# A transformer block in float32 halves: where GpSimd's elementwise work stands in the order

## Chip, cores and metric

One NeuronCore of a Trainium2 chip runs the whole kernel. The metric is the device time of one execution in microseconds, as the median of several runs.

## What is computed

A transformer block with adaptive layer norm, for one batch of 2048 rows of 512 values, all in float32. Six vectors of 512 come from the condition `c`; they scale, shift and gate.

```python
mod = (silu(c) @ w_mod).reshape(1, 6, 1, -1)
sa, ca, ga, sb, cb, gb = six vectors of mod
h = layernorm(x) * (1 + ca) + sa
q, k, v = split(h @ wqkv)                  # 32 heads of 16
p = softmax(q @ k.T * 16 ** -0.5)
x = x + ga * ((p @ v) @ wo)
h = layernorm(x) * (1 + cb) + sb
u = h @ w1 + b1                            # 1792 wide
x = x + gb * ((u * tanh(softplus(u))) @ w2)
```

## The kernel before

**Float32 products from parts.** A matrix product runs as three products of fp32r operands: each operand is split into a high part (a copy rounded to fp32r, `hi_copy`) and a low part (the rest, `lo_sub`), and high x high, high x low and low x high are added up in PSUM. So each intermediate that enters a product is split first, by a copy and a subtraction, mostly on GpSimd (`eng="p"`).

**Attention sets the beat.** The rows are cut into four query blocks of 512, the heads into eight groups of four: 32 iterations n = 8 qb + g. Each iteration has sixteen steps, T = 512 steps in all, and each step works on 128 keys: four products of scores (L506), their exponentials on ScalarE (L514, tile `pr`), the product with the values two steps later (L534), and, for a later iteration, four products (L470) whose row maxima VectorE reduces (L472, `mx`). Scores and maxima go through a ring of six PSUM banks. Each step is two half steps h = 2t and 2t + 1.

**An order written out by hand.** The schedule is manual: every engine runs its instructions in the order in which the program emits them. `at(h, f)` puts a function on the list of half step h, and the lists are run in order, each in the order in which it was filled. So "+13" says where an instruction stands in its engine's queue, not when it runs; what runs later is set by the waits. `clear(h)` only moves a half step out of a stretch of each iteration. SP issues all the transfers, in order; GpSimd runs its work in order too.

**Units beside the attention.** The other products are cut into units that are queued in a fixed order (`queue`) and emitted a few at a time beside the scores, on half the rows of the array each. A unit's `fin(h)` follows its last product and hangs the elementwise stages on the half steps behind it. There are these kinds:

- `qk_unit` projects 128 columns of q or k for 512 rows. ScalarE copies the bank into `ql` (L242), GpSimd makes the high part `qh` (L95) and turns `ql` into the low part (L98). `put`, some half steps later, stores them to DRAM in the layout in which the pairs of heads are loaded: for q two stores of `qh` and one of `ql` (L252), for k one of `qh` written twice (L256) and one of `ql` (L257). `qh` and `ql` have two buffers each. These units lie ahead of iteration 7's end.
- The MLP of query block qb, from iteration 8 (qb + 1) on: `wo_unit` (attention output, four row blocks), `tr_unit` (transposes after the layer norm), fourteen `up_unit` f = 0 to 13 (128 columns of the 1792 each, a slice), and `down_unit` (the product with w2 for a group of slices and 128 rows; its sum is added to `y` on GpSimd, L879, out of one buffer `yd`). In the order, slices 0 to 4 follow one another, slices 5 to 8 alternate with the first group's `down_unit`, of six products, and later slices with wider ones. An `up_unit` takes eight half steps, the first group's `down_unit` four. The fourth query block's MLP is a tail of its own.

**A slice's stages** (`mish`), for a unit whose `fin` is at h, outside the tail: bias on ScalarE (L728, tile `hb`), clamp on GpSimd (L734, into `ee`), exponential on ScalarE (L740), a product of two instructions on GpSimd (L748, L749), logarithm and inverse on ScalarE (L752, L755), the quotient of five instructions on GpSimd (L764 to L768), `place` (no instruction) and the split into `a_h` and `a_l` on GpSimd (L95, L98). The half steps behind h are in the list that the diff changes, from clamp to split.

**A group of heads is finished** in `evac(n)`, called at the end of step t1 = 16 (n + 1) + 1: ScalarE copies the accumulator to `ot` (L548). The sums of the exponentials go by DMA to `sm` (L559, `sums`), the four heads' rows to half of `od` (L563, `rows`), VectorE takes the reciprocal `rc` (L569), SP stores it to DRAM (`rscr`, L570) and loads it back, spread over the rows (`rb`, L572). When two groups (a pair, g odd) are there, GpSimd multiplies (L578) and splits the result into `o_hl` (L95, L98), which `wo_unit` reads. `od` and `rb` have one buffer each. With `hurry` (g = 7, the block's last heads) the steps stand closer, and the three instructions on one half step.

The order in the lists decides also what stands beside these: a pair of heads' k and q (`load_pair`, L293 and L302) at half step 32 (n - 2) + 9 or 15 and at 32 (n - 1), the values (L457), wo's four quarters for the next block (`w<-woscr`, L660, two of them when the fourth group's last unit is done), and the stores of the row maxima into `qa` (L495) at 32 n - 5.

Of the kernel before, what the change touches and what calls it, by code (L numbers as in the profile page):

```python
# [8 lines left out]
F32 = mybir.dt.float32  # L9
# [9 lines left out]
def adaln_block(ctx: ExitStack, tc: tile.TileContext, x, wqkv, wo, w1, b1, w2, c, w_mod, out):  # L19
    nc = tc.nc  # L20
    P = 128
    S, D = x.shape[1], x.shape[2]
# [5 lines left out]
    TB = 512  # L28
# [32 lines left out]
    rscr = dram.tile([NIT, 4, TB], F32, name="rscr")  # L61
# [24 lines left out]
    def dap(t, off, ap):  # L86
        return bass.AP(tensor=t.tensor, offset=t.offset + off, ap=ap)

    def hi_copy(eng, hi, src):
        if eng == "a":  # L90
            nc.scalar.copy(hi, src)
        elif eng == "v":
            nc.vector.tensor_copy(hi, src)
        else:
            nc.gpsimd.tensor_scalar(hi, src, 1.0, 0.0, op0=ALU.mult, op1=ALU.add)  # L95

    def lo_sub(eng, lo, src, hi):
        (nc.gpsimd if eng == "p" else nc.vector).tensor_sub(lo, src, hi.bitcast(F32))  # L98
# [12 lines left out]
    def mm3(acc, ah, al, bh, bl, late="a"):  # L111

        n = len(ah)
        seq = ((ah, bh), (ah, bl), (al, bh)) if late == "a" else ((ah, bh), (al, bh), (ah, bl))
        seq = [(l[k], r[k]) for l, r in seq for k in range(n)]
        for i, (l, r) in enumerate(seq):
            mm(acc, l, r, i == 0, i == len(seq) - 1)
# [36 lines left out]
    def bank(tag="ms"):  # L154
        return ring() if tag == "ring" else ps.tile([P, TB], F32, tag=tag, name="bk", bufs=1)
# [25 lines left out]
    def clear(h):  # L181

        return h if h < 60 or h % 32 < 25 else h - h % 32 + 34

    def at(h, f):

        hooks.setdefault(h, []).append(f)
# [38 lines left out]
    def qk_unit(kind, ct, tb, tag):  # L226

        wh, wl = slices[kind, ct]
        acc = bank(tag)
        ts_ = slice(tb * TB, (tb + 1) * TB)  # L230
        mm3(acc, [wh[:, k, :] for k in range(DK)], [wl[:, k, :] for k in range(DK)],
            [h_h[:, k, ts_] for k in range(DK)], [h_l[:, k, ts_] for k in range(DK)], "b")

        def fin(h=None):
            qh = qp.tile([P, TB], F32R, tag="qh", name="qh", bufs=2)
            ql = qp.tile([P, TB], F32R, tag="ql", name="ql", bufs=2)
            if h is None:
                hi_copy("a", qh, acc)
                lo_sub("v", ql, acc, qh)
            else:  # L240
                qf = ql.bitcast(F32)
                nc.scalar.copy(qf, acc)  # L242
                hi_copy("p", qh, qf)
                lo_sub("p", ql, qf, qh)
            scr, rows = (qscr, 50) if kind == 0 else (kscr, 48)

            def put():
                put_away.add((kind, ct, tb))
                o = 8 * ct * rows * S + tb * TB
                if kind == 0:  # L250
                    for r, src in enumerate((qh, qh, ql)):
                        nc.sync.dma_start(dap(scr, o + r * S, [[rows * S, 8], [3 * S, DH], [1, TB]]), src.bitcast(F32))  # L252
                    return
                hi = qh.bitcast(F32)
                twice = bass.AP(tensor=hi.tensor, offset=hi.offset, ap=[list(hi.ap)[0], [0, 2], [1, TB]])
                nc.sync.dma_start(dap(scr, o, [[3 * S, P], [2 * S, 2], [1, TB]]), twice)  # L256
                nc.sync.dma_start(dap(scr, o + S, [[3 * S, P], [1, TB]]), ql.bitcast(F32))  # L257

            put() if h is None else at(clear(h + (5 if h > 60 else 2)), put)
        return fin  # L260
# [265 lines left out]
    def pv(t):  # L526
        if not 0 <= t < T:
            return
        n, kc = divmod(t, 16)
        if kc == 0:  # L530
            accs[n] = bank("acc")
        for h in range(4):
            o = (kc * 4 + h) * VW
            nc.tensor.matmul(accs[n][32 * h:32 * h + 32, :], vgs[n][:, o:o + 32], pts.pop((t, h)),  # L534
                             start=(kc == 0), stop=(kc == 15))
        if kc == 15:
            evac(n)
# [4 lines left out]
    def evac(n):  # L542
        qb, g = divmod(n, G)
        t1 = 16 * (n + 1) + 1
        if g == 0:
            o_hl[qb] = [ap.tile([P, DK, TB], F32R, tag=f"o_{i}", name="o_hl", bufs=1) for i in range(2)]
        ot = ap.tile([P, TB], F32, tag="ot", name="ot", bufs=1)
        nc.scalar.copy(ot, accs.pop(n))  # L548
        if g % 2 == 0:
            st["od"] = ap.tile([P, TB], F32, tag="od", name="od", bufs=1)  # L550
            st["rb"] = ap.tile([P, TB], F32, tag="rb", name="rb", bufs=1)
        od, rb = st["od"], st["rb"]
        b = 64 * (g % 2)
        if n == NIT - 1:
            mst["last"] = (ot, od, rb)
            return
        sm = ap.tile([P, 16], F32, tag="sm", name="sm", bufs=2)
        def sums():
            nc.sync.dma_start(sm, ot[DH::32, :])  # L559

        def rows():
            for h in range(4):
                nc.sync.dma_start(od[b + 16 * h:b + 16 * h + 16, :], ot[32 * h:32 * h + DH, :])  # L563

        rc = ap.tile([P, 16], F32, tag="rc", name="rc", bufs=2)
        hurry = g == G - 1
        at(2 * t1 + 2, sums)
        at(2 * t1 + 3, rows)
        at(2 * t1 + (10 if hurry else 12), lambda: nc.vector.reciprocal(rc, sm))  # L569
        at(2 * t1 + (11 if hurry else 13), lambda: nc.sync.dma_start(rscr[n], rc))  # L570
        at(2 * t1 + (13 if hurry else 17),
           lambda: nc.sync.dma_start(rb[b:b + 64, :], dap(rscr, n * 4 * TB, [[TB, 4], [0, DH], [1, TB]])))  # L572
        if g % 2 == 1 or n == NIT - 2:
            r = slice(0, P if g % 2 else 64)

            oh, ol = o_hl[qb]
            k, d = 2 * t1 + (29 if g == 1 else 17 if hurry else 23), 0 if hurry else 2
            at(k, lambda: nc.gpsimd.tensor_mul(od[r], od[r], rb[r]))  # L578
            at(k + d, lambda: hi_copy("p", oh[r, g // 2, :], od[r]))
            at(k + 2 * d, lambda: lo_sub("p", ol[r, g // 2, :], od[r], oh[r, g // 2, :]))  # L580
# [85 lines left out]
    def load_w1(f):  # L666
        return load_split("w1", 2, w1scr[f])
# [42 lines left out]
    def up_mms(acc, w, hh, hl):  # L710
        mm3(acc, [w1v(w, 0, k) for k in range(DK)], [w1v(w, 1, k) for k in range(DK)],
            [hh[:, k, :] for k in range(DK)], [hl[:, k, :] for k in range(DK)], "b")
# [67 lines left out]
    def idle(h):  # L780

        return h is not None and 2 * (T - PRO) + 2 < h <= 2 * T
# [5 lines left out]
    def block(qb, t0):  # L788
# [60 lines left out]
        def up_unit(f, tag):  # L849
            w = w1s.pop(f)  # L850
            acc = bank(tag)
            up_mms(acc, w, *hx)
            act[f], (bias, *stages) = mish(f, acc, False)

            def fin(h):
                bias(idle(h))
                for i, s in zip((1, 3, 4, 9, 13, 13, 16, 18) if f < 5 else (1, 5, 6, 9, 13, 13, 16, 18), stages):
                    at(h + i, s)
                done["a", f] = h + 20
                if f + 2 < FT:  # L860
                    w1s[f + 2] = load_w1(f + 2)
                elif qb + 1 < len(blocks):
                    blocks[qb + 1]["w1"][f + 2 - FT] = load_w1(f + 2 - FT)
            return fin
# [492 lines left out]
```

## Time and profile before

| | |
|---|---|
| median of 3 runs | 1781.03 us (1779.73 to 1781.47) |
| profiled execution | 1780.51 us, span 1778.7 us |
| granted TensorE clock, mean | 0.984 |
| TensorE busy | 1701.5 us, 96% |
| VectorE busy | 1428.9 us, 80% |
| ScalarE busy | 1344.0 us, 76% |
| GpSimd busy | 887.3 us, 50% |
| moved by DMA | 240.03 MB, mean 135 GB/s |

In the profile PE is TensorE's products and PEld its weight loads, DVE VectorE, ACT ScalarE, POOL GpSimd, SP SyncE; L472 is line 472 of the kernel. A row of the list of waits has the waiting engine, line and tile, the one waited for, then the microseconds in total, how often, and the longest. A row of the timeline has the start from the span's start, the duration, engine, line, operation, tiles (out<-in), shapes and how many; in square brackets the idle time of the engine just before, and what ended it. A row of the chain has start, duration and what ran. A row of a stretch has the stretch, its length, the busy time of PE, PEld, DVE, ACT and POOL with the number of instructions, the granted TensorE clock, the share of DMA, and GB/s. A group row has the busy time and the mean in ns, then the idle time before and what ended it.

### The profile page before, as it was taken

Reading aid. Unit: us, or ns where it says so; the run is one execution under the profiler, and the core shown is the slowest. Engines: PE = TensorE matmul, PEld = TensorE weight load, DVE = VectorE, ACT = ScalarE, POOL = GpSimd, SP = SyncE. Lnnn points to the kernel's source line nnn. Section 1 sums busy time; section 2 is a strip of 40 time slices with the busy share of each in tenths; the row PEclk is TensorE's granted clock in tenths of the full one; section 3 lists DMA queues with packets and bytes.
Section 4 is the critical chain, followed back from the end, with each engine's and each line's share of the span. In section 5 each row is a group of like instructions: output and inputs, shape, how many; then the busy total and the mean of one; then the engine's idle time right before and its main releaser. Section 6 shows DMA issues by size and latency. Waiting matters only on the chain.

```text
span 1778.7 us, 32821 instructions
## 1 busy us (share of the span) xinstructions
PE 1701.5 (96%) x12236; PEld 935.5 (53%) x12236; DVE 1428.9 (80%) x2352; ACT 1344.0 (76%) x2605; POOL 887.3 (50%) x868
## 2 busy tenths in 40 slices
PE   7999999999899999999999999999999999999998
PEld 5755655455344544555545544455545544554676
DVE  6988888888888877888878877888878877881367
ACT  6257777777779887788869877788878877788464
POOL 5255224656113496644523585655423676646452
PEclk9999999999999998999999999999999999999999
DMA  7776467777824443335342633344343524332252
GB/s 255 185 228 199 125 163 242 216 230 214 269 67 112 100 100 97 88 102 126 105 94 70 176 88 99 86 127 116 91 100 100 163 74 117 74 117 102 95 213 71
DMA packets 113992, 240.03 MB, mean 135 GB/s; under 512 B 24048, under 2 KB 49648, under 8 KB 107784
## 3 DMA queue, kind: packets, MB, share of 16 engines
q1 hardware_dynamic: 113832, 237.92, 47.1%
q8 instruction: 97, 1.59, 0.4%
q14 instruction: 63, 0.52, 0.1%
HBM read 179.95 MB, written 51.44 MB: 130 GB/s over the span
## 4 chain that ended last, share of the span: by engine, by line
PE 72%; POOL 10%; DMA 8%; ACT 4%; DVE 2%; issue 2%; SPq 2%; POOLq 0%; ACTq 0%; DVEq 0%
PE bk L534 23%; PE ring L470 18%; PE ring L506 17%; PE bk L132 8%; DMA qscr<-ql 2%; ACT pr L514 2%; PE ring L126 2%; DMA rb<-rscr 2%; POOL ee L734 2%; PE ring L1060 1%; POOL hb L768 1%; PE bk L126 1%; POOL rr L766 1%; POOL ee L764 1%; POOL hb L767 1%
## 5 line engine op out<-in xcount | busy, mean ns | idle before, releaser
L472 DVE TENSOR_REDUCE mx<-ring 128x1 f32<-128x512 f32 x2048 | 1279.4, 684 | 237.1 <-PE bk L132 136.7
L514 ACT ACTIVATE pr<-ring 128x512 f32<-128x512 f32 x2048 | 1091.5, 610 | 252.1 <-PE bk L132 152.3
L470 PE MATMUL ring<-ka,qa 64*128 64x512 f32 x2048 | 791.5, 432 | 6.5 <-ACT pr L514 5.9
L506 PE MATMUL ring<-qa,ka 64*128 64x512 f32 x2048 | 731.7, 403 | 23.8 <-ACT pr L514 22.5
L470 PEld LDWEIGHTS ring<-ka,qa 64*128 64x128 f32 x2048 | 371.4, 187 | 424.4 <-DVE mx L472 354.3
L534 PE MATMUL bk<-pr,vg 128*32 128x512 f32 x4096 | 552.5, 611 | 0.0
L506 PEld LDWEIGHTS ring<-qa,ka 64*128 64x128 f32 x2048 | 378.9, 188 | 129.4 <-ACT pr L514 67.8
L132 PE MATMUL bk<-h,w 64*128 64x512 f32 x1008 | 290.6, 419 | 8.6 <-ACT yd L878 7.1
L132 PE MATMUL bk<-w,a_h 64*128 64x512 f32 x576 | 196.7, 421 | 0.6 <-ACT pr L514 0.6
L132 PEld LDWEIGHTS bk<-h,w 64*128 64x128 f32 x1008 | 177.0, 189 | 21.5 <-ACT yd L878 8.0
L534 PEld LDWEIGHTS bk<-pr,vg 128*32 128x32 f32 x4096 | 81.7, 108 | 132.0 <-issue 124.5
L764 POOL TENSOR_TENSOR ee<-ee,rr 128x512 f32<-128x512 f32 x42 | 53.8, 1281 | 189.8 <-ACT rr L755 189.8
L132 PE MATMUL bk<-w,a_l 64*128 64x512 f32 x288 | 114.7, 398 | 0.0
L132 PEld LDWEIGHTS bk<-w,a_h 64*128 64x128 f32 x576 | 96.9, 187 | 8.5 <-ACT pr L514 3.3
L734 POOL TENSOR_SCALAR ee<-hb 128x512 f32<-128x512 f32 x42 | 62.4, 1485 | 66.7 <-ACT hb L728 64.0
L132 PE MATMUL bk<-w,o_hl 64*128 64x512 f32 x288 | 83.5, 420 | 9.1 <-POOL o_hl L95 7.2
L879 POOL TENSOR_TENSOR y<-yd,y 128x512 f32<-128x512 f32 x50 | 64.2, 1283 | 52.8 <-ACT yd L878 51.2
L98 POOL TENSOR_TENSOR a_l<-hb,a_h 128x512 fp32r<-128x512 f32 x53 | 71.6, 1351 | 4.4
L132 PEld LDWEIGHTS bk<-w,o_hl 64*128 64x128 f32 x288 | 50.7, 190 | 14.5 <-POOL o_hl L95 8.5
L132 PE MATMUL bk<-h_h,wl 64*128 64x512 f32 x168 | 56.8, 418 | 0.0
L132 PEld LDWEIGHTS bk<-w,a_l 64*128 64x128 f32 x288 | 53.7, 187 | 4.0
L766 POOL TENSOR_TENSOR rr<-rr,ee 128x512 f32<-128x512 f32 x42 | 54.1, 1287 | 3.5
(204 smaller groups left out, 1789.2 us busy)
## 6 DMA issues: line engine op xcount, KB each, us to landing
ka<-kscr SPq DMA_DIRECT2D x124, 384.0 KB
w<-w2scr SPq DMA_DIRECT2D x56, 512.0 KB
w<-w1scr SPq DMA_DIRECT2D x46, 512.0 KB
vg<-vscr SPq DMA_DIRECT2D x32, 552.0 KB
qa<-qscr SPq DMA_DIRECT2D x124, 100.0 KB
kscr<-qh SPq DMA_DIRECT2D x16, 512.0 KB
qscr<-qh SPq DMA_DIRECT2D x32, 256.0 KB
hl<-in_B_w SPq DMA_DIRECT2D x28, 256.0 KB
```

The costliest lines, as they stand in the source:

```text
L98: (nc.gpsimd if eng == "p" else nc.vector).tensor_sub(lo, src, hi.bitcast(F32))
L126: nc.tensor.matmul(acc, l, r, start=start, stop=stop)
L132: i = nc.tensor.matmul(acc, l[64 * g:64 * g + 64], r[64 * g:64 * g + 64], start=start, stop=stop)
L470: nc.tensor.matmul(pm, qt[64 * s:64 * s + 64, qs * P:(qs + 1) * P], kt[64 * s:64 * s + 64, kb * TB:(kb + 1) * TB], start=True, stop=True)
L472: return nc.vector.tensor_reduce(out=mxs[n][:, s, 4 * j + qs, kb:kb + 1], in_=pm, op=ALU.max, axis=AX.X)
L506: nc.tensor.matmul(p_, kt[64 * s:64 * s + 64, kc * P:(kc + 1) * P], qt[64 * s:64 * s + 64, :], start=True, stop=True)
L514: e = nc.scalar.activation(pr, p_, AF.Exp, scale=SCALE)
L534: nc.tensor.matmul(accs[n][32 * h:32 * h + 32, :], vgs[n][:, o:o + 32], pts.pop((t, h)), start=(kc == 0), stop=(kc == 15))
L734: nc.gpsimd.tensor_scalar_min(buf("ee", 2), b["hb"], HCAP)
L764: nc.gpsimd.tensor_mul(ee, ee, rr)
L766: nc.gpsimd.tensor_sub(rr, rr, ee)
L879: nc.gpsimd.tensor_add(y[i], yd, y[i])
```

## The change

Three things are moved; no instruction is added or taken away. The quotient of slices 4 to 13 stands on half step h + 14 in place of h + 13. Of the groups of heads, the block's last (g = 7) has its reciprocal, store, load and split five or six half steps sooner; the second pair (g = 1) has its split seven later, and for that the rows of the third group (g = 2) go to `od` nine half steps later. And the stores of a projection that is computed beside the attention begin with the low part.

```diff
                 if kind == 0:
-                    for r, src in enumerate((qh, qh, ql)):
+                    for r, src in ((2, ql), (0, qh), (1, qh)) if h else ((0, qh), (1, qh), (2, ql)):
                         nc.sync.dma_start(dap(scr, o + r * S, [[rows * S, 8], [3 * S, DH], [1, TB]]), src.bitcast(F32))
                     return
...
-                nc.sync.dma_start(dap(scr, o, [[3 * S, P], [2 * S, 2], [1, TB]]), twice)
-                nc.sync.dma_start(dap(scr, o + S, [[3 * S, P], [1, TB]]), ql.bitcast(F32))
+                both = (dap(scr, o, [[3 * S, P], [2 * S, 2], [1, TB]]), twice),                     (dap(scr, o + S, [[3 * S, P], [1, TB]]), ql.bitcast(F32))
+                for to, src in reversed(both) if h else both:
+                    nc.sync.dma_start(to, src)
...
         at(2 * t1 + 2, sums)
-        at(2 * t1 + 3, rows)
-        at(2 * t1 + (10 if hurry else 12), lambda: nc.vector.reciprocal(rc, sm))
-        at(2 * t1 + (11 if hurry else 13), lambda: nc.sync.dma_start(rscr[n], rc))
-        at(2 * t1 + (13 if hurry else 17),
+        at(2 * t1 + (12 if g == 2 else 3), rows)
+        at(2 * t1 + (5 if hurry else 12), lambda: nc.vector.reciprocal(rc, sm))
+        at(2 * t1 + (6 if hurry else 13), lambda: nc.sync.dma_start(rscr[n], rc))
+        at(2 * t1 + (8 if hurry else 17),
            lambda: nc.sync.dma_start(rb[b:b + 64, :], dap(rscr, n * 4 * TB, [[TB, 4], [0, DH], [1, TB]])))
...
-            k, d = 2 * t1 + (29 if g == 1 else 17 if hurry else 23), 0 if hurry else 2
+            k, d = 2 * t1 + (36 if g == 1 else 11 if hurry else 23), 0 if hurry else 2
             at(k, lambda: nc.gpsimd.tensor_mul(od[r], od[r], rb[r]))
             at(k + d, lambda: hi_copy("p", oh[r, g // 2, :], od[r]))
             at(k + 2 * d, lambda: lo_sub("p", ol[r, g // 2, :], od[r], oh[r, g // 2, :]))
...
-                for i, s in zip((1, 3, 4, 9, 13, 13, 16, 18) if f < 5 else (1, 5, 6, 9, 13, 13, 16, 18), stages):
+                for i, s in zip((1, 3, 4, 9, 13, 13 if f < 4 else 14, 16, 18) if f < 5 else (1, 5, 6, 9, 13, 14, 16, 18), stages):
                     at(h + i, s)
```

## The prediction

> **What bounds the kernel now.** I read the page first (busy shares, chain), then the list of waits, then ScalarE's copies of the attention accumulators (L548), one for each iteration of sixteen steps, which tell where time is lost; last the GpSimd, ScalarE and TensorE rows around each loss.
>
> ```profile
> PE 1701.5 (96%) x12236; PEld 935.5 (53%) x12236; DVE 1428.9 (80%) x2352; ACT 1344.0 (76%) x2605; POOL 887.3 (50%) x868
> PE 72%; POOL 10%; DMA 8%; ACT 4%; DVE 2%; issue 2%; SPq 2%; POOLq 0%; ACTq 0%; DVEq 0%
> ACT ee L740 <- POOL ee L734: 38.6, 15, 2.7
> ACT ql L242 <- DMA qscr<-ql: 9.3, 5, 3.1
> SPq L563 <- POOL o_hl L98: 11.2, 3, 3.8
> ```
>
> TensorE bounds it (72% of the chain), so a gain has to be time in which TensorE stands or runs slowly. GpSimd, half idle, still has 10% of the chain: fifteen times ScalarE stands for GpSimd's clamp, 2.6 us each. In the next rows the iteration is the distance from one copy to the next.
>
> ```profile
> 635.41 0.60 ACT L548 COPY ot<-bk 128x512 f32<-128x512 f32 x1
> 744.32 0.62 ACT L548 COPY ot<-bk 128x512 f32<-128x512 f32 x1
> 790.04 0.61 ACT L548 COPY ot<-bk 128x512 f32<-128x512 f32 x1
> 835.67 0.63 ACT L548 COPY ot<-bk 128x512 f32<-128x512 f32 x1
> 881.43 0.61 ACT L548 COPY ot<-bk 128x512 f32<-128x512 f32 x1
> 935.63 0.61 ACT L548 COPY ot<-bk 128x512 f32<-128x512 f32 x1
> 984.57 0.62 ACT L548 COPY ot<-bk 128x512 f32<-128x512 f32 x1
> 1276.68 0.61 ACT L548 COPY ot<-bk 128x512 f32<-128x512 f32 x1
> 1329.13 0.60 ACT L548 COPY ot<-bk 128x512 f32<-128x512 f32 x1
> ```
>
> A quiet iteration takes 835.67 - 790.04 = 45.63 us, so a half step (a 32nd) 1.426 us. From 635.41 two iterations take 108.91, 17.65 over quiet: the five clamp waits of the first MLP block lie there, 3.5 us each. Three blocks make 53.0 us. The iteration from 881.43 takes 54.20, the one from 1276.68 takes 52.45: the block changes. An iteration with three transposes of normalised rows costs (984.57 - 935.63 - 45.63)/3 = 1.1 for each, and the block changes hold one; so 7.5 and 5.7 are lost there otherwise.
>
> **The quotient behind the clamp, and the second pair's split.** Slice 7 of the first block, its bias at 695.75; the quotient at 698.88 is slice 6's.
>
> ```profile
> 695.75 0.69 ACT L728 ACTIVATE hb<-bk,b1c 128x512 f32<-128x512 f32 x1
> 698.88 1.28 POOL L764 TENSOR_TENSOR ee<-ee,rr 128x512 f32<-128x512 f32 x1 [7.96 <-ACT rr L755]
> 704.94 1.48 POOL L734 TENSOR_SCALAR ee<-hb 128x512 f32<-128x512 f32 x1
> 706.46 0.63 ACT L740 ACTIVATE ee<-ee 128x512 f32<-128x512 f32 x1 [2.57 <-POOL ee L734]
> 710.39 1.28 POOL L749 TENSOR_TENSOR ee<-ee,rr 128x512 f32<-128x512 f32 x1
> 706.00:708.00 2.00, 0.38 (x2) 0.26 (x2) 0.59 (x1) 1.54 (x4) 1.92 (x3) 0.92 0.90 193
> 708.00:710.00 2.00, 2.00 (x12) 1.50 (x10) 0.69 (x1) 1.67 (x5) 1.92 (x3) 0.50 0.89 234
> ```
>
> GpSimd idles 7.96 us waiting for slice 6's inverse, although slice 7's bias is there from 696.44; then come the five instructions of the quotient (6.06), then the clamp. ScalarE stands 2.57 us for it with the attention's exponentials queued behind, TensorE's banks are not freed, and the granted clock falls to 0.50 afterwards, which makes 3.5 of 2.6. From slice 4 the slices that alternate with one narrow product are twelve half steps apart, so the clamp (bias + 1) and the old quotient (+ 13) share a half step and the older goes first. With + 14 the clamp runs at 696.5, in idle time, and the quotient still starts at 698.88, set by the inverse. No instruction is added. The clamp's wait goes at slices 5 to 8.
>
> What is late next: behind the clamp stand a row block's accumulation (L879), the split of slice 6 and slice 7's own product, which ScalarE's logarithm waits for. They move up by the clamp's 1.56 only: the product ends at 711.67 - 1.56 = 710.11. The exponential would run at 706.46 - 2.57 = 703.89, the logarithm four half steps on, at 709.59. So a wait of 0.5 us stands where 2.57 stood. ScalarE is busy 76% of the span, so of a step (2.85 us) some 0.7 us is idle on average, less beside a slice; I bound a residual between 0 (absorbed) and 1.5 (its size and a clock drop) and take 0.3, nearer to the first. Where slices stand sixteen half steps apart (from 8 on) the order does not change, and the half step later costs nothing: the inverse sets the start.
>
> Slice 4 waits for another reason: slices 0 to 4 are eight half steps (11.4 us) apart, about what GpSimd needs for one, and the second head pair's three instructions fall in between.
>
> ```profile
> 629.41 1.29 POOL L578 TENSOR_TENSOR od<-od,rb 128x512 f32<-128x512 f32 x1
> 632.63 0.62 POOL L95 TENSOR_SCALAR o_hl<-od 128x512 fp32r<-128x512 f32 x1
> 639.15 1.30 POOL L98 TENSOR_TENSOR o_hl<-od,o_hl 128x512 fp32r<-128x512 f32 x1
> 640.54 1.48 POOL L734 TENSOR_SCALAR ee<-hb 128x512 f32<-128x512 f32 x1
> 642.06 0.63 ACT L740 ACTIVATE ee<-ee 128x512 f32<-128x512 f32 x1 [2.71 <-POOL ee L734]
> 657.07 1.28 POOL L764 TENSOR_TENSOR ee<-ee,rr 128x512 f32<-128x512 f32 x1 [1.80 <-ACT rr L755]
> 664.64 0.63 ACT L740 ACTIVATE ee<-ee 128x512 f32<-128x512 f32 x1 [2.49 <-POOL ee L734]
> 668.56 1.27 POOL L749 TENSOR_TENSOR ee<-ee,rr 128x512 f32<-128x512 f32 x1
> ```
>
> Moved from + 29 to + 36 they stand behind that clamp, which ends at 642.02 - 3.21 = 638.8; the exponential wants it at 642.06 - 2.71 = 639.35. The wait goes, by half a microsecond. But the 3.21 us arrive in slice 5's stretch: from that clamp to the end of slice 5's product GpSimd worked from 640.54 to 669.83 with 1.80 idle, 27.5 us; with the three it is 30.7, from 637.3 to 668.0. Slice 5's exponential, with slice 4's 2.9 us gone, is due at 664.64 - 2.49 - 2.9 = 659.2, its logarithm 5.7 later, at 664.9. So the logarithm of slice 5 waits 3.1 us, more than its exponential did. I price it at 3.7 (between 0, if GpSimd catches up, and 4.2 with the clock drop), nearest to the fifteen that stand in the trace. Per block 3.7 + 3 x 0.3 = 4.6 remains of 17.65; in three blocks 13.8 of 53.0. **Gain 39.2.**
>
> [...]
>
> The rows of the third group (g == 2) move to + 12 on SP because they overwrite what the later split reads. SP stood 3.7 us a block for that already (L563, above); behind it on the queue stand the reciprocals' store and load, w1's loads, and the next row maxima (qa<-mt) thirteen half steps on, 18 us, which covers it. Price 0; without the cover up to 3.7 a block. A gain is excluded, as nobody on the path waits for these rows.
>
> **The block's last heads, sooner.**
>
> ```profile
> L132 PE MATMUL bk<-w,o_hl 64*128 64x512 f32 x288 | 83.5, 420 | 9.1 <-POOL o_hl L95 7.2 <-POOL o_hl L98 1.9
> 908.28 0.50 PE L132 MATMUL bk<-w,o_hl 64*128 64x512 f32 x1 [3.22 <-POOL o_hl L95]
> 882.06 0.62 SPq L559 DMA_DIRECT2D sm<-ot  x1
> 882.72 3.55 SPq L563 DMA_DIRECT2D od<-ot  x4
> 892.64 0.24 DVE L569 RECIPROCAL rc<-sm 128x16 f32<-128x16 f32 x1
> 1288.15 3.27 DMA rscr<-rc
> 895.42 10.69 DMA rb<-rscr
> 896.13 0.39 SPq L660 DMA_DIRECT2D w<-woscr  x1
> ```
>
> TensorE idles 9.1 us for these heads in three block changes. With the clock behind it the second and third cost 7.5 and 5.7 (above), the first I put at 2, since two waits like the one at 908.28, each with one for the low part behind it, leave some 2 of the 9.1: 15.2. Now the reciprocal comes five half steps sooner, 892.64 - 7.1 = 885.5, 3.4 us after the sums' transfer was issued. VectorE would stand if that is late; I take 0, bound it at 1 us for each. SP issues the store when its four row transfers are out, at 886.3; 3.27 later (the longest of the rows) the broadcast, at 889.9. It also passes the loads of a head pair and of w<-woscr, which made it 10.69 long: it was queued behind them, and they now queue behind 128 KB. Even at 10.69 it lands by 900.6, and three instructions (3.2) end at 903.8, before TensorE needs them at 908.28 - 3.22 = 905.06. On GpSimd, one accumulation stands behind the moved product and waits for its own copy anyway. Late next is wo's last quarter (issued 896.13, right after the broadcast that landed at 906.1). SP reaches it about 2.5 us sooner, so it lands at some 904 to 905: price 0 to 2 in two blocks, I take 0.7 in all. **Gain 14.5.**
>
> **Low parts first.**
>
> ```profile
> 452.08 0.58 ACT L242 COPY ql<-bk 128x512 f32<-128x512 f32 x1 [3.06 <-DMA qscr<-ql]
> 94.06 0.96 PE L126 MATMUL bk<-h_h,wh 128*128 128x512 f32 x3 [1.27 <-ACT ql L242]
> GB/s 255 185 228 199 125 163 242 216 230 214 269 67 112 100 100 97 88 102 126 105 94 70 176 88 99 86 127 116 91 100 100 163 74 117 74 117 102 95 213 71
> ```
>
> ScalarE's copy of a projection waits until the low part of two projections ago, third in its queue, is stored. Two stores of 256 KB ahead of it take 0.52 MB / 230 GB/s (the ninth slice) = 2.3 us, which is about the waits (9.3 us in five). First in the queue, it lands before it is wanted. The high part's buffer comes free later, for which GpSimd waits beside other work; SP now waits for GpSimd's low part ahead of all three, 1.3 us at most, and seldom, since its stores are issued long after. Bounds 0 (the transfers' rate sets the pace of the stretch) and 9.3 (all the waits, at full price); I take 5, the middle, because the queue restarts at each iteration's reciprocal; in the prologue, TensorE's 1.3. **Gain 6.3.**
>
> **Sum.** 39.2 + 14.5 + 6.3 = 60.0. The profiled execution took 1780.51 us, so 1720.5; the median of the runs is 0.5 above it: 1721.
>
> **Rivals.** (a) The wait only changes its place: slices 6 to 8 wait for the logarithm's input as long as they did for the clamp. Then of 53.0 only slice 4's 10.5 goes, and with 14.5 and 6.3 it is 1749. For it: the logarithm is already 0.5 late by my working; against it: that is a fifth of the old wait. (b) Slice 5's logarithm is in time as well, and the residuals vanish: 13.8 less, 1707. Against: GpSimd's 30.7 us have no gap to give. (c) Slower: the same twelve logarithms wait W each, at W + 1 with the clock; they eat all three gains from 12 (W + 1) = 73.8, W = 5.2; at 6 it is 1791. That takes 4.7 us more GpSimd work in each slice than the rows show, against 7.96 idle before each quotient. (d) wo's weights come as late as the heads did at the two later changes: 13 less gain, 1734, in my own range.
>
> **Numbers.** My forecast with (d), 1704 to 1740: 0.78. (a) and mixtures with it, 1740 to 1760: 0.12. Below 1704, (b) with the bound of the stores: 0.04. No change (gains returned): 0.02. (c) 0.04. Range 1704 to 1748. No change means within 0.2%, 3.6 us, about what this measurement can tell; faster 0.94, same 0.02, slower 0.04.
>
> **What would show it.** Right: the fifteen clamp waits are gone; the iterations after 635 take 95 to 101 us for two instead of 108.9; a wait of L752 for L749 appears, about 3 us at slice 5 of each block and under 1 at 6 to 8; no wait of L132 for o_hl; rb<-rscr lands within 5 us at the block changes; no wait of L242 for qscr<-ql above 1 us. Wrong: L752 waiting 2 us or more at slices 6 to 8; slice 4 still waiting; L132 waiting for w<-woscr; VectorE waiting for sm.

## The result, and the profile after

The changed kernel takes 1725.32 us (median of 4 runs, 1724.28 to 1726.11) against 1781.25 before (median of 4); the ratio is 0.9678, with a 95% interval of 0.9651 to 0.9705. The forecast was 1721. The profiled execution took 1725.0 us, 55.5 less than that of before. All lines behind L257 are one higher now: L549 is the copy that was L548.

The page, the list of waits, and the copies that mark the iterations, of the changed kernel:

```profile
span 1723.2 us, 32800 instructions
PE 82%; POOL 6%; DMA 5%; ACT 3%; DVE 2%; issue 1%; SPq 1%; ACTq 0%; DVEq 0%; POOLq 0%
```
```profile
ACT rr L753 <- POOL ee L750: 12.7, 12, 3.0
```
```profile
631.45 0.60 ACT L549 COPY ot<-bk 128x512 f32<-128x512 f32 x1
679.81 0.59 ACT L549 COPY ot<-bk 128x512 f32<-128x512 f32 x1
726.43 0.62 ACT L549 COPY ot<-bk 128x512 f32<-128x512 f32 x1
863.56 0.61 ACT L549 COPY ot<-bk 128x512 f32<-128x512 f32 x1
910.33 0.61 ACT L549 COPY ot<-bk 128x512 f32<-128x512 f32 x1
```

TensorE has 82% of the chain where it had 72%, GpSimd 6 where it had 10. The fifteen waits for the clamp are gone; twelve waits of the logarithm (L753) for GpSimd's product have come in their place, 12.7 us in all for 38.6. The first MLP block's two iterations take 726.43 - 631.45 = 94.98 us (108.91 before), the block change from 863.56 takes 46.77 (54.20). In this table, made from such rows of both profiles, the whole difference can be found:

| stretch | before | after | difference | forecast |
|---|---|---|---|---|
| iterations 11 and 12, 19 and 20, 27 and 28 (slices 4 to 8 of three blocks) | 326.91 | 288.06 | -38.8 | -39.2 |
| iterations 8, 16, 24 (block changes) | 155.58 | 140.25 | -15.3 | -14.5 |
| start to the first copy | 159.76 | 160.29 | +0.5 | -1.3 |
| iterations 4 to 7 (projections and their stores) | 192.35 | 190.15 | -2.2 | -5 |
| the rest | 944.1 | 944.4 | +0.3 | 0 |

Two terms came within a microsecond. The third, the stores, was expected to bring 6.3 and brought 1.7 here, 4.6 us less; the profiled execution, 1725.0, lies 4.5 above the 1720.5 forecast for it.

How slices 5 and 7 of the first block look on ScalarE and GpSimd now (the first row is slice 4's clamp):

```profile
633.49 1.48 POOL L735 TENSOR_SCALAR ee<-hb 128x512 f32<-128x512 f32 x1
651.30 1.49 POOL L735 TENSOR_SCALAR ee<-hb 128x512 f32<-128x512 f32 x1
652.87 1.27 POOL L765 TENSOR_TENSOR ee<-ee,rr 128x512 f32<-128x512 f32 x1
662.70 1.26 POOL L750 TENSOR_TENSOR ee<-ee,rr 128x512 f32<-128x512 f32 x1
664.00 0.72 ACT L753 ACTIVATE rr<-ee,two 128x512 f32<-128x512 f32 x1 [2.98 <-POOL ee L750]
697.55 1.29 POOL L750 TENSOR_TENSOR ee<-ee,rr 128x512 f32<-128x512 f32 x1
698.88 0.72 ACT L753 ACTIVATE rr<-ee,two 128x512 f32<-128x512 f32 x1 [0.49 <-POOL ee L750]
```

Slice 5's clamp (L735, 651.30) stands ahead of slice 4's quotient (L765). Slice 5's logarithm waits 2.98 us for the product that ends at 663.96; slice 7's waits 0.49.

At the block changes, from the changed kernel's timeline of VectorE, SP and GpSimd (two rows of the first change, three of the second), and its group of wo's products:

```profile
497.77 0.59 SPq L573 DMA_DIRECT2D rb<-rscr  x1
502.04 1.29 POOL L579 TENSOR_TENSOR od<-od,rb 128x512 f32<-128x512 f32 x1 [37.69 <-DMA rb<-rscr]
867.88 0.24 DVE L570 RECIPROCAL rc<-sm 128x16 f32<-128x16 f32 x1
869.88 0.60 SPq L573 DMA_DIRECT2D rb<-rscr  x1
875.48 1.29 POOL L579 TENSOR_TENSOR od<-od,rb 128x512 f32<-128x512 f32 x1
L132 PE MATMUL bk<-w,o_hl 64*128 64x512 f32 x288 | 79.6, 409 | 0.0
```

At the first change GpSimd waits for the broadcast until 4.3 us after its issue. At the second the product with the reciprocals starts 5.6 us after the issue, without a wait in brackets (it stands behind an accumulation), where the broadcast alone took 10.69; in the trace its 128 KB have moved by 873.2, 3.4 us after the issue, and at the third change by 2.7 us after it. So it lands within the 5 us of the prediction. TensorE waits 0.0 us for these heads in place of 9.1.

One wait has grown, on the queue of SP:

```profile
SPq L564 <- POOL a_h L95: 45.2, 3, 15.4
```

The third group's rows now stand on SP until the second pair's split has read `od`, 15 us a block where it was 3.7. (In the first block the split's last instruction, L98 into `o_hl`, ends at 649.28 and the rows go out at 649.30; `a_h`, which the row names, is what GpSimd runs next.) The prediction had 18 us of cover behind them and a price of 0: TensorE does not wait for a row maximum (qa<-mt) anywhere behind 480 us, so the price held, with little of the cover left.

### The profile page after: what moved, and what is told of

Its sections match the earlier page's. It is cut to its first block, busy times and chain, and to the rows that moved or that the text cites. A ratio compares the mean times of both kernels' runs of the same rounds, so it can differ in the third digit from the quotient of the medians.

```text
span 1723.2 us, 32800 instructions
## 1 busy us (share of the span) xinstructions
PE 1677.6 (97%) x12236; PEld 930.9 (54%) x12236; DVE 1427.8 (83%) x2352; ACT 1341.0 (78%) x2605; POOL 887.3 (51%) x868
## 4 chain that ended last, share of the span: by engine, by line
PE 82%; POOL 6%; DMA 5%; ACT 3%; DVE 2%; issue 1%; SPq 1%; ACTq 0%; DVEq 0%; POOLq 0%
PE bk L535 26%; PE ring L471 21%; PE ring L507 19%; PE bk L132 8%; PE bk L126 3%; PE ring L126 2%; ACT pr L515 2%; DMA qscr<-ql 1%; PE ring L1061 1%; DMA w2scr<-hl 1%; POOL y L880 1%; POOL a_l L98 1%; DMA ka<-kscr 1%; DMA wma<-in_w_mod 1%; DVE mx L473 1%
## 5 line engine op out<-in xcount | busy, mean ns | idle before, releaser
L471 PE MATMUL ring<-ka,qa 64*128 64x512 f32 x2048 | 782.1, 427 | 8.3 <-ACT pr L515 7.4
L507 PE MATMUL ring<-qa,ka 64*128 64x512 f32 x2048 | 719.9, 398 | 11.5 <-DMA qa<-mt 6.8
L471 PEld LDWEIGHTS ring<-ka,qa 64*128 64x128 f32 x2048 | 366.9, 184 | 421.8 <-DVE mx L473 355.3
L507 PEld LDWEIGHTS ring<-qa,ka 64*128 64x128 f32 x2048 | 373.4, 185 | 115.6 <-ACT pr L515 47.8
L132 PE MATMUL bk<-h,w 64*128 64x512 f32 x1008 | 283.1, 412 | 1.5 <-ACT pr L515 1.5
L132 PEld LDWEIGHTS bk<-h,w 64*128 64x128 f32 x1008 | 172.5, 185 | 11.2 <-ACT pr L515 4.4
L735 POOL TENSOR_SCALAR ee<-hb 128x512 f32<-128x512 f32 x42 | 62.4, 1486 | 102.5 <-ACT hb L729 100.5
L765 POOL TENSOR_TENSOR ee<-ee,rr 128x512 f32<-128x512 f32 x42 | 53.8, 1280 | 117.0 <-ACT rr L756 116.8
L132 PEld LDWEIGHTS bk<-w,a_h 64*128 64x128 f32 x576 | 95.6, 185 | 9.2 <-ACT pr L515 3.3
L98 POOL TENSOR_TENSOR a_l<-hb,a_h 128x512 fp32r<-128x512 f32 x53 | 71.7, 1352 | 4.4
L753 ACT ACTIVATE rr<-ee,two 128x512 f32<-128x512 f32 x56 | 40.6, 726 | 21.4 <-POOL ee L750 12.7
L750 POOL TENSOR_TENSOR ee<-ee,rr 128x512 f32<-128x512 f32 x42 | 54.1, 1288 | 3.5
L769 POOL TENSOR_TENSOR hb<-hb,rr 128x512 f32<-128x512 f32 x42 | 54.2, 1289 | 3.3
```

The lines of the kernel that those rows point to most:

```text
L132: i = nc.tensor.matmul(acc, l[64 * g:64 * g + 64], r[64 * g:64 * g + 64], start=start, stop=stop)
L471: nc.tensor.matmul(pm, qt[64 * s:64 * s + 64, qs * P:(qs + 1) * P], kt[64 * s:64 * s + 64, kb * TB:(kb + 1) * TB], start=True, stop=True)
L507: nc.tensor.matmul(p_, kt[64 * s:64 * s + 64, kc * P:(kc + 1) * P], qt[64 * s:64 * s + 64, :], start=True, stop=True)
L735: nc.gpsimd.tensor_scalar_min(buf("ee", 2), b["hb"], HCAP)
L750: nc.gpsimd.tensor_mul(ee, ee, rr)
L769: nc.gpsimd.tensor_mul(hb, hb, rr)
```

## Experiments

The diffs show only the lines or arguments that change; `...` marks what is left out.

**The quotient alone, and the second pair alone.** By the prediction's working, three instructions of 3.2 us cost about the same whether they stand ahead of slice 4's clamp or behind it, since slice 5 pays then. The theory says that order alone is worth nearly all; its rival, that the parts add up as the prediction priced slice 4 (10.5).

```diff
-  ... zip((1, 3, 4, 9, 13, 13, 16, 18) if f < 5 else (1, 5, 6, 9, 13, 13, 16, 18), stages)
+  ... zip((1, 3, 4, 9, 13, 13 if f < 4 else 14, 16, 18) if f < 5 else (1, 5, 6, 9, 13, 14, 16, 18), stages)
```

> Only the quotient's half step (+14 from slice 4 on), on the kernel before. Theory one (the three od instructions cost about the same wherever they stand between slices 3 and 5): slice 4's clamp still waits 2.7 us in each block, but slice 5's logarithm, with no od instructions behind it, waits only about 0.5 us like those of 6 to 8. A block keeps some 3.2 + 4 x 0.3 = 4.4 of its 17.5 us, so the gain is about 39 us, as large as quotient and split together: 1742. Theory two (the sum of the prediction read part by part, the split brings slice 4's 10.5 us): without it the gain is 28 to 29 us, 1752, and slice 5's logarithm waits about 3 us here too.

Measured: 1743.27 us against 1783.14 before, ratio 0.9782 (0.9755 to 0.9809), 38.9 us by the ratio. From ScalarE's timeline of the first block:

```profile
643.91 0.63 ACT L740 ACTIVATE ee<-ee 128x512 f32<-128x512 f32 x1 [2.70 <-POOL ee L734]
671.53 0.72 ACT L752 ACTIVATE rr<-ee,two 128x512 f32<-128x512 f32 x1 [0.42 <-POOL ee L749]
```

Slice 4's clamp still waits 2.70, but slice 5's logarithm only 0.42. The three blocks take 35.6 us less than before, against 38.8 for both parts together. Theory one holds. How much of the 3.2 us between the two is the split's isn't shown: in this profile iteration 27 alone takes 1.2 us more than 11 and 19, at a granted clock of 0.93 for their 0.97.

```diff
-  at(2 * t1 + 3, rows)
+  at(2 * t1 + (12 if g == 2 else 3), rows)
   ...
-  k, d = 2 * t1 + (29 if g == 1 else 17 if hurry else 23), 0 if hurry else 2
+  k, d = 2 * t1 + (36 if g == 1 else 17 if hurry else 23), 0 if hurry else 2
```

> Only the second pair's split at +36 and the third group's rows at +12, on the kernel before. Theory one: slice 4's clamp wait goes, slice 5's clamp wait grows from 2.5 to about 3.7 us, because the three instructions now stand ahead of it; gain 3 x 2, about 6 us: 1775. Theory two: slice 4's share goes and slice 5's wait stays, gain 10.5: 1770.5. Rival: SP stands longer at the third group's rows and a wait of TensorE for qa appears: no gain.

Measured: 1774.12 us, ratio 0.9958 (0.9940 to 0.9977), a gain of 4 to 11 us, which doesn't tell 6 from 10.5. The waits do, from its list of waits and its timeline:

```profile
ACT ee L740 <- POOL ee L734: 33.1, 12, 3.4
```
```profile
664.43 0.63 ACT L740 ACTIVATE ee<-ee 128x512 f32<-128x512 f32 x1 [3.32 <-POOL ee L734]
685.33 0.63 ACT L740 ACTIVATE ee<-ee 128x512 f32<-128x512 f32 x1 [2.56 <-POOL ee L734]
```

Slice 4's wait is gone (twelve are left), and slice 5's has grown from 2.49 to 3.32, as theory one says. The blocks take 12.1 us less, more than the 5.5 us of waiting saved and nearer to theory two's 10.5 than to theory one's 6. But equal waits cost unequal times here (see the clock below): the granted clock over iterations 11, 19 and 27 is 0.97, 1.00 and 1.00 in this profile, and 0.94, 0.91 and 0.94 in that of before. So the size is no argument for either. 35.6 and 12.1 add up to 47.7; together they bring 38.8.

**The second pair where GpSimd is free.** If slice 5 waits because of those three instructions, they belong behind slice 5's product, where GpSimd idles.

```diff
-  at(2 * t1 + (12 if g == 2 else 3), rows)
+  at(2 * t1 + (28 if g == 2 else 3), rows)
   ...
-  at(2 * t1 + (8 if hurry else 17),
+  at(2 * t1 + (8 if hurry else 24 if g == 2 else 17),
      ...
-  k, d = 2 * t1 + (36 if g == 1 else 11 if hurry else 23), 0 if hurry else 2
+  k, d = 2 * t1 + (54 if g == 1 else 11 if hurry else 23), 0 if hurry else 2
```

> The changed kernel, with the second pair's split later still: at +54, behind slice 5's product, where GpSimd idles 4 us before slice 6's clamp; the third group's rows at +28 and its broadcast at +24, since they write what that split reads. Theory (slice 5's logarithm waits 3 us because the three od instructions, 3.2 us, stand between slice 4's clamp and slice 5's product): its wait falls below 0.6 us and nothing else waits; 2.3 to 3.9 us a block, so 8 to 11 us below the changed kernel, 1715. Rival one: they then hold up slice 6 by as much, 0 gain, 1725. Rival two: SP stands at the later rows and broadcast and the row maxima come late: slower than 1725.

Measured: 1715.32 us against 1782.46, ratio 0.9620 (0.9592 to 0.9648). The list of waits and ScalarE's and GpSimd's timeline of it:

```profile
ACT rr L753 <- POOL ee L750: 5.0, 12, 0.5
```
```profile
663.07 0.72 ACT L753 ACTIVATE rr<-ee,two 128x512 f32<-128x512 f32 x1 [0.43 <-POOL ee L750]
662.99 1.28 POOL L579 TENSOR_TENSOR od<-od,rb 128x512 f32<-128x512 f32 x1
665.06 1.29 POOL L98 TENSOR_TENSOR o_hl<-od,o_hl 128x512 fp32r<-128x512 f32 x1
667.10 1.49 POOL L735 TENSOR_SCALAR ee<-hb 128x512 f32<-128x512 f32 x1 [0.74 <-ACT hb L729]
```

Slice 5's wait is 0.43 like the others', and the three instructions end before slice 6's bias is there. The blocks' six iterations take 277.4 us, 10.7 less than in the changed kernel. What is left over the quiet iterations of this profile (45.72 each) is 3.1 us for twelve waits: 0.26 each, the prediction's 0.3.

**And the logarithm half a step later.**

```diff
-  ... else (1, 5, 6, 9, 13, 14, 16, 18), stages)
+  ... else (1, 5, 6, 10 if f < 9 else 9, 13, 14, 16, 18), stages)
```

> As the one before, and the logarithms of slices 5 to 8 one half step later (+10). Theory: the residual waits of 0.3 to 0.5 us go, at 0.3 us each: 2 to 4 us below the one before, about 1712. Rival: ScalarE absorbs them already, no difference; or the inverse and with it the quotient move back, and the split of slices 5 to 8 delays a product with w2: slower.

Measured: 1710.01 us, ratio 0.9589 (0.9563 to 0.9615). No wait of ScalarE for GpSimd is left in the slices of its profile, and the blocks' iterations are quiet: from the timeline,

```profile
631.10 0.60 ACT L549 COPY ot<-bk 128x512 f32<-128x512 f32 x1
676.69 0.59 ACT L549 COPY ot<-bk 128x512 f32<-128x512 f32 x1
722.58 0.62 ACT L549 COPY ot<-bk 128x512 f32<-128x512 f32 x1
```

45.59 and 45.89 us. All six take 274.4, 3.0 less than the version before, as expected. The median falls by 5.3, since iterations 4 to 7, whose code is the same, took 189.3 us in this profile and 192.2 in the other. It is the lowest median of the study; two versions further down are not told apart from it.

**The last heads alone.**

```diff
-  at(2 * t1 + (10 if hurry else 12), lambda: nc.vector.reciprocal(rc, sm))
-  at(2 * t1 + (11 if hurry else 13), lambda: nc.sync.dma_start(rscr[n], rc))
-  at(2 * t1 + (13 if hurry else 17),
+  at(2 * t1 + (5 if hurry else 12), lambda: nc.vector.reciprocal(rc, sm))
+  at(2 * t1 + (6 if hurry else 13), lambda: nc.sync.dma_start(rscr[n], rc))
+  at(2 * t1 + (8 if hurry else 17),
      ...
-  k, d = 2 * t1 + (29 if g == 1 else 17 if hurry else 23), 0 if hurry else 2
+  k, d = 2 * t1 + (29 if g == 1 else 11 if hurry else 23), 0 if hurry else 2
```

> Only the hurried reciprocal, store, load and split of the block's last heads, on the kernel before. Theory: the three block changes lose their waits for o_hl, 15 us: 1766, with the broadcast landing within 5 us of its issue. Rival: wo's last quarter is late in its place, gain 2 to 8 us: 1773 to 1779.

Measured: 1771.37 us, ratio 0.9931 (0.9904 to 0.9959), 12 us where 15 were expected. In its profile wo's products idle 0.0 us, and iterations 8, 16 and 24 take 139.9 us, 15.7 less than before: the term is confirmed, and wo's last quarter is not late. The median shows less; in the profiled run iterations 4 to 7, whose code is that of before up to the end of 7, took 195.8 us where the profile of before has 192.4, and the three MLP blocks, with the same clamp waits, 331.3 where it has 326.9.

**The low parts first, alone.**

```diff
-  for r, src in enumerate((qh, qh, ql)):
+  for r, src in ((2, ql), (0, qh), (1, qh)) if h else ((0, qh), (1, qh), (2, ql)):
   ...
-  nc.sync.dma_start(dap(scr, o, ...), twice)
-  nc.sync.dma_start(dap(scr, o + S, ...), ql.bitcast(F32))
+  both = (dap(scr, o, ...), twice), (dap(scr, o + S, ...), ql.bitcast(F32))
+  for to, src in reversed(both) if h else both:
+      nc.sync.dma_start(to, src)
```

> Only the low parts stored first, on the kernel before. Theory one (the transfers' rate sets the pace of iterations 4 to 7): the waits of ScalarE for qscr go from 9 to about 2 us, but TensorE's wait for the row maxima qa<-mt grows from 1.1 to 4 to 6 us: gain 0 to 2.5 us, 1779 to 1781. Theory two (the gain was eaten by the other three parts): 6 us here, 1775, and the wait for qa<-mt stays at about 1 us.

Measured: 1778.80 us, ratio 0.9973 (0.9957 to 0.9989): 2 to 8 us, between the theories. What TensorE and ScalarE wait for, from the waits of 300 to 480 us: before, then low parts first (where ScalarE has no row for qscr), then the whole change.

```profile
ACT ql L242 <- DMA qscr<-ql: 8.4, 4, 3.1
PE ring L506 <- DMA qa<-mt: 1.1, 1, 1.1
```
```profile
PE ring L507 <- DMA qa<-mt: 5.8, 3, 3.7
```
```profile
ACT ql L242 <- DMA qscr<-ql: 1.7, 2, 1.0
PE ring L507 <- DMA qa<-mt: 5.7, 3, 2.6
```

ScalarE's waits went, as the prediction said. But TensorE now waits for the row maxima, which stand behind the same stores: 1.1 became 5.8. In iteration 4 it reaches them 40.7 us after the copy that starts the iteration, in place of 42.0, and they come after 44.3, in place of 43.2.

**With fewer transfers.** Of the prepared weights w2, the stores are left out in the changed kernel and in that of before.

```diff
-  at(clear(h + 9), lambda: nc.sync.dma_start(...))
+  if gate != 1:
+      at(clear(h + 9), lambda: nc.sync.dma_start(...))
   ...
-  return load_split("w2", NW, w2scr[f])
+  return load_split("w2", NW, w1scr[f])
```

> The changed kernel without the stores of the fourteen w2 preparations (512 KB each, in iterations 5 to 7); w1's prepared weights are loaded in their place, so the MLP's second product is with other weights, at the same sizes and times. Theory (the transfers' rate is what makes the row maxima late): TensorE's waits for qa<-mt in iterations 6 and 7 (3.1 us) go, the one in iteration 4 stays: 3 to 4 us below the changed kernel, 1721.5. Rival (they are late because of their place in SP's order): the waits stay, 1725.

> The kernel before with the same stores left out. Theory: ScalarE's waits for qscr<-ql in iterations 6 and 7 (2.05 and 3.06 us) go without any new order: 4 to 6 us below before, 1776. Rival: they stay, since the low part is still third in its queue: 1781.

Measured: 1718.27 us, ratio 0.9644 (0.9616 to 0.9671), where 1721.5 was expected, and 1776.62 us, ratio 0.9971 (0.9953 to 0.9988), for 1776. With the new order the wait for qa<-mt falls from 5.7 to 1.0 us:

```profile
PE ring L507 <- DMA qa<-mt: 1.0, 1, 1.0
```

Two of the three waits, 1.77 and 1.31 us, stand behind the stores that are left out, and they are gone. The third, 2.64 us with the stores and 1.04 without, ends at 344.41, ahead of the first of these stores (363.68), where both kernels are the same: this part of the fall is a difference from run to run. In the old order two of ScalarE's waits, 2.05 and 3.06 us, fall to 0.89 and 0.84; a third, of 3.4 us, stands ahead of the stores as well. Iterations 6 and 7 take 89.9 us in the new order, for 92.0 to 95.0 in its five profiles with the stores, and 91.1 in the old, for 95.6 to 96.4. So the load on the queue makes these waits, and in either order most of them go with it. The first theory for the kernel before held in part, as 1.7 of these 5.1 us stay. Whether it is the bytes, the number of transfers outstanding or the time in which SP issues them isn't told apart.

**The stores' order in the fastest version.** Once with the old order throughout, once with the old order in the prologue only.

> The fastest version (gap_and_log) with the stores in the old order: the high parts first. Theory one (the transfers' rate sets the pace; the new order trades ScalarE's waits for qscr<-ql for TensorE's waits for qa<-mt and brings 2 to 4 us in iterations 4 to 7, and costs 1 us ahead of iteration 0): 1712 to 1713, iterations 4 to 7 together 193 to 196 in place of 189.3, the start up to the first copy of an accumulator at 159 to 160. Theory two (the new order is worth the 6 us of the prediction): 1716, the gain being in both stretches.

> The fastest version with the low parts first only from half step 1 on; in the prologue's stretch (negative half steps) the high parts first as before. Theory (in the prologue the new order puts GpSimd behind the store of the high part, whose 512 KB land last, in place of ScalarE behind the low part's, and costs about 1 us): the start up to the first copy of an accumulator takes 159 to 160 in place of 161, in all 1709. Rival (that stretch differs from chip to chip by as much): 161, 1710.

Measured: 1711.30 us, ratio 0.9602 (0.9574 to 0.9630), and 1711.39 us, ratio 0.9602 (0.9577 to 0.9626), against 0.9589 for the fastest version: the times don't tell them apart. The stretches of the profiles tell a little more:

| | old order | new order |
|---|---|---|
| iterations 4 to 7, five profiles each | 192.4, 194.1, 194.3, 195.8, 193.4 | 190.2, 190.2, 192.2, 189.3, 188.6 |
| start to the first copy | 159.8, 158.9, 158.6, 160.5, 162.0, 160.4 | 161.8, 160.3, 160.2, 161.0 |

In iterations 4 to 7 the two don't overlap, and the means differ by 3.9 us. The waits of 300 to 480 us don't overlap either: ScalarE's for qscr are 7.9 to 9.6 us in the five profiles of the old order and 0 to 1.7 in those of the new, TensorE's for qa<-mt 1.1 to 2.1 and 5.0 to 6.1. On average 8.3 us of the first go and 4.3 of the second come. At the start the two orders do overlap, and no gain or loss is shown; the sixth value of the old order is the version that keeps it in the prologue. The microsecond expected of it stays open, as the same code differs by 3.5 us from run to run there. Of the two theories for the old order, the first gave 193 to 196 us for iterations 4 to 7, and 193.4 were measured; its start of 159 to 160 was missed with 162.0.

## Why the prediction was right or wrong

**The quotient's order: right, with its waits.** It gave 0.5 us for the logarithms of slices 6 to 8 and the rows have 0.49, 0.49 and 0.27; it gave 3.1 for slice 5 and the three blocks have 2.98, 2.95 and 2.98. What hit it is the count of GpSimd's work from slice 4's clamp to the end of slice 5's product: 30.7 us without a gap by the prediction, 30.5 in the profile (633.49 to 663.96), without a gap. Of 53.0 us lost, 13.8 were to remain; 14.3 do (over the 45.63 of a quiet iteration).

That 38.8 came so near to 39.2 is partly luck. With the same fifteen waits the three blocks took 326.9 us in the profile of before, and 324.9, 327.2 and 331.3 in those of fewer transfers, the low parts alone and the last heads alone; with the changed kernel's order they took 288.1 and, with fewer transfers, 289.4. By these the gain lies anywhere from 35.5 to 43.2.

**The second pair's split: the mechanism right, its share of the gain easily misread.** The 10.5 us that rival (a) leaves for slice 4 are paid back at slice 5: with the quotient's order alone the blocks gain 35.6, with both 38.8, and the difference is no larger than what the clock does from run to run. What the move lacked was a place that is free; at +54 it is worth 10.7 more.

**The last heads: right.** 14.5 forecast, 15.3 measured; by block change 2, 7.5 and 5.7 were counted, and 2.2, 7.4 and 5.7 came. The 0.7 taken off for wo's weights and the bound for VectorE's wait were not needed at the two later changes; VectorE stood once for sm, 0.60 us, at the first. That is one of the prediction's signs of being wrong, and a small one: iteration 8 takes 46.7 us here, and 46.3 in five later profiles with the same last heads and no such wait. In one more, the version with the old order in the prologue, VectorE stood 1.71 us there and iteration 8 took 47.9, so the bound of 1 us was too low.

**The low parts: a term that was mis-sized.** The step that failed is the choice of 5 us between 0 and 9.3, argued with a queue that restarts at each iteration, and the 1.3 for the prologue. The stretches show 3.9 in place of the 5, and no gain in the prologue. The bound of 0 had the reason in it, the load on the queue: the low part came sooner, and the row maxima behind it then became what TensorE waits for. The prediction asked what follows on SP where it moved the third group's rows, but not here.

**Rival (a)** is out (slices 6 to 8 wait a fifth), **(b)** did not come with this change and is what the later split and the later logarithm bring together, **(c)** and **(d)** did not occur: TensorE never waits for wo's weights.

**On the clock.** Slice 5's wait is the same in the three blocks but not its price: iteration 11 takes 48.36 us, iteration 19 takes 49.88, iteration 27 takes 49.96. From the changed kernel, TensorE's first product behind the stall in the first two blocks, and stretches of 2 us around it (the granted clock stands behind the five engines' busy times):

```profile
665.25 0.50 PE L471 MATMUL ring<-ka,qa 64*128 64x512 f32 x1 [2.48 <-ACT pr L515]
1038.85 0.50 PE L471 MATMUL ring<-ka,qa 64*128 64x512 f32 x1 [2.45 <-ACT pr L515]
663.00:665.00 2.00, 0.00 (x0) 0.00 (x0) 0.42 (x2) 1.00 (x2) 0.96 (x1) 1.00 0.01 2
665.00:667.00 2.00, 1.75 (x12) 1.19 (x14) 1.19 (x2) 1.91 (x5) 0.00 (x0) 1.00 0.02 5
1038.00:1040.00 2.00, 1.15 (x6) 0.66 (x8) 0.61 (x1) 1.90 (x5) 0.00 (x0) 0.93 0.02 6
1040.00:1042.00 2.00, 2.00 (x14) 1.16 (x16) 1.16 (x3) 1.50 (x3) 0.00 (x0) 0.50 0.01 2
```

In the first block the clock stays at 1.00 behind the stall, in the second it falls to 0.50, though TensorE idles 2.48 and 2.45 us (ScalarE waits 2.98 and 2.95). So in these rows the length of the stall does not settle the clock behind it; what does is shown by no run here. Over 45.63 for a quiet iteration the three blocks pay 2.7, 4.2 and 4.3 us, 3.8 on average. The prediction's 3.7 is such an average, and nothing in its working tells which of the three stalls would cost more.

## What to carry to other kernels

Where an engine in the middle of a chain serves several items at once, put the short instruction that releases another engine ahead of the long one that nobody waits for yet; then add up that engine's work from this release to the next one that somebody waits for, because there the wait comes back (here 2.98 us at slice 5). A burst that is moved out of one crowded stretch has to go to where the engine's rows show idle time, not just behind the next release (here the move to idle time brought 10.7 us more). And when a transfer is moved ahead in a loaded queue, look up what TensorE waits for behind it: about half of the time won at one transfer here was lost at the next, while the load stayed.

## What was not expected of the hardware

Equal stalls cost 2.7 or 4.2 us by the granted clock (1.00 over iteration 11, 0.97 over iteration 19), so that the same fifteen clamp waits (38.5 to 38.6 us in all) cost the three blocks 53.1 us in the profile of before and 57.5 in that of the last heads alone (over six iterations of 45.63); over iterations 11, 19 and 27 the clock was 0.94, 0.91 and 0.94 in the one and 0.91 each time in the other. And the stretch full of transfers, iterations 4 to 7, took 192.4 to 195.8 us with the same order of stores, a spread nearly as large as the 3.9 us that the order is worth there.
